# Attention and gated-MLP block in float32 pairs: the low-weight pass of a 64-channel rest as two 64-row matmuls on separate halves of the array

## The chip, the cores and the metric

The kernel runs on one core of a Trainium2 chip. The metric is the device time of one execution in microseconds (us). The kernel before was run three times: 1588.62 us median, 1587.64 lowest, 1589.95 highest.

The engines are TensorE (PE in the profile; its weight loads are listed apart as PEld), VectorE (DVE), ScalarE (ACT), GpSimd (POOL) and SyncE (SP, which issues most loads).

## The reference, cut to what matters

One transformer block over 2048 tokens of 576 channels, in float32:

```python
def reference(A_x, A_wqkv, A_wo, B_x, B_w_gate, B_w_up, B_w_down):
    def _A_ref(x, wqkv, wo):            # H = 32 heads of 18, window of 8 keys, dilation 2
        qkv = (x @ wqkv) ...            # x: (1, 2048, 576), wqkv: (576, 1728)
        idx = pos[:, None] - off[None, :]       # off = 0, 2, ..., 14; masked where negative
        logits = jnp.einsum("bhsd,bhswd->bhsw", q, kg) * scale
        attn = _softmax(logits, axis=-1)
        o = jnp.einsum("bhsw,bhswd->bhsd", attn, vg)
        return ... @ wo
    def _B_ref(x, w_gate, w_up, w_down):        # 576 -> 4608 -> 576
        return (sigmoid(x @ w_gate) * (x @ w_up)) @ w_down
    h = x + _A_ref(_layernorm(x), A_wqkv, A_wo)
    return h + _B_ref(_layernorm(h), B_w_gate, B_w_up, B_w_down)
```

## The kernel before

**Numbers as pairs.** A float32 matrix product is made of products of float32r parts. An operand is split (`split`, lines 103 to 105): ScalarE writes the rounded value `hi`, VectorE writes `lo`, the source less `hi`. A product is then hi times hi, lo times hi, and hi times lo; the product of the two low parts is left out.

**The rest of 64 channels.** The 576 channels are four chunks of 128 and a rest of 64. The rest is held twice, on rows 0 to 63 and on rows 64 to 127. For the tokens (`split_rest`, lines 107 to 109) ScalarE writes the rounded values to all 128 rows, and VectorE replaces rows 64 to 127 by the low parts: the fifth chunk of `th` is 64 rows of hi and 64 rows of lo. The weights are held twice as well, and `wh[:, 4]` and `wl[:, 4]` each have the same 64 rows on both halves. So one 128-row matmul of `th[:, 4]` with `wh[:, 4]` makes hi times hi and lo times hi together, and a second one with `wl[:, 4]` makes hi times lo, and lo times lo beside it.

**QKV.** The tokens are taken by parity (the window has dilation 2) and by half: four blocks of 512 tokens, each of four tiles of 128. The 32 heads are four groups, so the weights of a group are 576 by 432 (q, k and v of eight heads). `qkv(b, g, T, w)` (line 377) does one block and one group: for each of its four tiles, `tok_major` (line 144) makes 14 matmuls of 128 rows by 432 columns into one accumulator `acc` of PSUM, 12 for the four chunks (line 150), one with `wh[:, 4]` (line 152) and one with `wl[:, 4]` (line 153). ScalarE then copies the accumulator to `ev` (line 384), and after the fourth tile three DMAs on ScalarE's queue write q, k and v to DRAM (lines 388 to 390). There are 16 calls, 64 tiles. Five buffers `acc` are shared with the transposes of the layer norm's rest (`ln1`, line 349) and with the output projection.

**Order.** Everything is unrolled, and the order of each engine is settled when the program is built, from the program's order and from priorities (`tc.high_priority`). The generators are stepped by hand. `qkv` yields after each tile, and between two yields one or more steps of the attention (`att_all`, line 399) are taken, whose arithmetic is on VectorE: multiply by the keys (line 182), reduce (186), softmax, multiply by the values (208), adds (214 to 219). In the first blocks a tile of the layer norm is stepped as well, with five transposes on TensorE (139 and 143), a split on ScalarE and VectorE (104, 105) and one of the rest (108, 109).

The calls run in the order (block, group) (0,0), (0,1), (1,0), (2,0), (3,0), (1,1), (0,2), (2,1), (3,1), half of (1,2), (0,3), the other half, (2,2), (3,2), (1,3), and then half of (2,3). Behind the last matmul of that half (`passes[-1]`) the output projection of block 0 is started (`front`, `proj_j`): transposes of the attention's result `o`, a split, products with `wo`, the layer norm of the sum, transposes, splits, and a spill of the result to DRAM (`xscr[0]`, line 505). The other half of (2,3) and (3,3) are stepped between its parts.

**MLP.** Then come 36 hidden tiles of 128 for each pair of blocks, with matmuls of 512 columns (609, 616) and of 288 (723). The attention and projection of the other blocks go on under them.

Of the kernel before, what the change touches and what calls it, by code (L numbers as in the profile page):

```python
# [17 lines left out]
AF = mybir.ActivationFunctionType  # L18
ALU = mybir.AluOpType
AX = mybir.AxisListType  # L20

P = 128
# [8 lines left out]
NS = 4  # L31
# [7 lines left out]
NQ = 3 * CG  # L39
# [21 lines left out]
def kernel(ctx, tc, x, wqkv, wo, wmlp, out):  # L61
    nc = tc.nc
    dve, act, pool, pe, sp = nc.vector, nc.scalar, nc.gpsimd, nc.tensor, nc.sync
# [34 lines left out]
    def f32(ap):  # L98
        return ap.bitcast(F32)
# [3 lines left out]
    def split(hi, lo, src):  # L103
        act.activation(hi, src, AF.Copy)  # L104
        splits.append(dve.tensor_tensor(lo, src, f32(hi), ALU.subtract))  # L105

    def split_rest(t, src):
        act.activation(t, src, AF.Copy)
        dve.tensor_tensor(t[64:128], src[64:128], f32(t[64:128]), ALU.subtract)  # L109

    def pads(g):
        for e in range(2):
# [5 lines left out]
    def ln_j(xj, xn, on_act):  # L118
        bs = sm.tile([P, 2, 6], F32, bufs=4, name="bs")
        mv = sm.tile([P, 2], F32, bufs=4, name="mv")  # L120
        rstd = sm.tile([P, 1], F32, bufs=4, name="rstd")
        for k in range(2):
            dve.bn_stats(bs[:, k], xj[:, k * DH2:(k + 1) * DH2])
        dve.bn_aggr(mv, bs)
        dve.tensor_scalar(rstd, mv[:, 1:2], EPS, None, ALU.add)
        pool.tensor_tensor(rstd, rstd, mhalf, ALU.pow)
        if on_act:
            nm = sm.tile([P, 1], F32, bufs=4, name="nm")
            dve.tensor_scalar(nm, mv[:, 0:1], -1.0, None, ALU.mult)
            act.activation(xn[:, :D], xj, AF.Identity, bias=nm)  # L130
            act.activation(xn[:, :D], xn[:, :D], AF.Copy, scale=rstd)
            act.activation(xn[:, D:DX], xn[:, DM:D], AF.Copy)
        else:
            dve.tensor_scalar(xn[:, :D], xj, mv[:, 0:1], rstd, ALU.subtract, ALU.mult)
            dve.tensor_copy(xn[:, D:DX], xn[:, DM:D])

    def tr_main(ps, xn):
        for c in range(4):
            pe.transpose(ps[:, c * P:(c + 1) * P], xn[:, c * P:(c + 1) * P], ident)
        return ps.rearrange("p (c n) -> p c n", c=4)  # L140

    def tr_rest(ps, xn):
        pe.transpose(ps[:, :P], xn[:, DM:DX], ident)
        return ps[:, :P]

    def tok_major(ps, n, th, tl, js, wh, wl):
        k = 0
        for c in range(4):
            for a, m in ((th, wh), (tl, wh), (th, wl)):
                pe.matmul(ps[:, :n], a[:, c, js], m[:, c], start=k == 0, stop=False)  # L150
                k += 1
        pe.matmul(ps[:, :n], th[:, 4, js], wh[:, 4], start=False, stop=False)  # L152
        return pe.matmul(ps[:, :n], th[:, 4, js], wl[:, 4], start=False, stop=True)  # L153

    behind = [None]

# [83 lines left out]
    def proj_j(bank, t, wos, th, tl, xn_tile, put, order=(0, 1)):  # L240
        oj = t[0]
        pv = tr_main(bank(), oj)
        with tc.high_priority(HI):
            split(th[:, 0:4], tl, pv)
        yield
        pv = tr_rest(bank(), oj)
        with tc.high_priority(HI):
            split_rest(th[:, 4], pv)
        yield
        for i in order:  # L250
            ps = bank()
            tok_major(ps, DH2, th, tl, slice(0, P), *wos[i])
            hs = t[1][:, i * DH2:(i + 1) * DH2]
            with tc.high_priority(HI):
                dve.tensor_tensor(hs, hs, ps[:, :DH2], ALU.add)
            yield
        xn = xn_tile()
        with tc.high_priority(HI):
            ln_j(t[1], xn, False)
        yield  # L260
        pv = tr_main(bank(), xn)
        with tc.high_priority(HI):
            put(pv, slice(0, 4))
        yield
        pv = tr_rest(bank(), xn)
        with tc.high_priority(HI):
            put(pv.unsqueeze(1), slice(4, 5))
        yield
# [18 lines left out]
    def th_tile():  # L287
        return xt.tile([P, 5, TB], F32R, tag="th", bufs=3, name="th")

    def tl_tile():  # L290
        return xt.tile([P, 4, TB], F32R, tag="tl", bufs=4, name="tl")

    def x_half(raw, rest):
        t = tl_tile() if rest is None else th_tile()
        split(t[:, 0:2], t[:, 2:4], raw)
        if rest is not None:
            split_rest(t[:, 4], rest)
        return t
# [17 lines left out]
    def mm_tile():  # L316
        return psp.tile([P, 512], F32, tag="mm", bufs=3, name="mm")

    def acc_tile():
        return psp.tile([P, 512], F32, tag="acc", bufs=5, name="acc")  # L320

    def tok_tile(shape=(P, NS, DX)):
        return stk.tile(list(shape), F32, tag="tok", bufs=2, name="tok")

    def th3_tile(dt):
        return sar.tile([P, 5, TB], dt, tag="th3", name="th3")

    def ev_tile(shape):
        return sar.tile(shape, F32, tag="ev", bufs=2, name="ev")
# [8 lines left out]
    def ln1(b, xb):  # L338
        th = th3_tile(F32R) if b == 3 else th_tile()
        tl = tl_tile()  # L340
        yield th, tl
        xn = tok_tile()
        for j in range(NS):
            js = slice(j * P, (j + 1) * P)
            pri = 2 * HI if b == 0 else HI if b > 1 else 0
            with tc.high_priority(pri):
                ln_j(xb[:, j], xn[:, j], b > 1)
            pv = tr_main(mm_tile(), xn[:, j])
            pr = tr_rest(acc_tile(), xn[:, j])
            with tc.high_priority(pri):  # L350
                split(th[:, 0:4, js], tl[:, :, js], pv)
                split_rest(th[:, 4, js], pr)
            yield

    def raw_w(g):
        if g == 3:
            wr = sah.tile([P, NS, D], F32, bufs=2, name="h").rearrange("p j d -> p (j d)")
            wr = wr[:, :QC].rearrange("p (c n) -> p c n", c=5)
        else:
            wr = swo.tile([P, 5, NQ], F32, tag="wo", name="wr")  # L360
        for c in range(5):
            sp.dma_start(wr[:, c], wqkv[g][:, c * NQ:(c + 1) * NQ])
        return wr

    def qkv_w(g, wr=None):
        w = saw.tile([P, 2, 5, NQ], F32R, tag="qw", bufs=2, name="qw")
        for c in range(5):
            if wr is None:
                ws = sas.tile([P, NQ], F32, tag="wst", bufs=3, name="ws")
                sp.dma_start(ws, wqkv[g][:, c * NQ:(c + 1) * NQ])  # L370
            else:
                ws = wr[:, c]
            with tc.high_priority(3 * HI if g == 0 else HI):
                split(w[:, 0, c], w[:, 1, c], ws)
        return w

    def qkv(b, g, T, w):
        e, hf = BLOCKS[b]
        ev = ev_tile([P, 3, NS, CG])
        for j in range(NS):  # L380
            ps = acc_tile()
            passes.append(tok_major(ps, NQ, *T, slice(j * P, (j + 1) * P), w[:, 0], w[:, 1]))
            with tc.high_priority(HI):
                act.activation(ev[:, :, j], ps[:, :NQ].rearrange("p (t c) -> p t c", t=3), AF.Copy)  # L384
            yield
        r0 = LP + hf * TB
        with tc.high_priority(HI):
            act.dma_start(qscr[b][g], ev[:, 0].rearrange("p j c -> p (j c)"))
            for t, s in ((1, kscr), (2, vscr)):
                act.dma_start(s[e][g][r0:r0 + TB, :].rearrange("(p j) c -> p (j c)", p=P),  # L390
                              ev[:, t].rearrange("p j c -> p (j c)"))
        emitted.add((b, g))
# [4 lines left out]
    passes = []  # L397
# [24 lines left out]
    T = []  # L422

    def norm_under(b, xb, call, n):
        gl = ln1(b, xb)
        T.append(next(gl))
        for _ in call:
            step(ag, n)
            next(gl, END)
            step(ag, n)  # L430
        drain(gl)

    def heads(order, ws, n):
        for b, g in order:
            for _ in qkv(b, g, T[b], ws[g]):
                step(ag, n)

    xb = load_x(0)
    w = [qkv_w(0, raw_w(0))]
    gl = ln1(0, xb)  # L440
    T.append(next(gl))
    run(gl, qkv(0, 0, T[0], w[0]))
    w.append(qkv_w(1))
    xb = load_x(1)
    pads(0)
    norm_under(1, xb, qkv(0, 1, T[0], w[1]), 0)
    pads(1)
    xb = load_x(2)
# [79 lines left out]
    last = passes[-1]  # L528
# [376 lines left out]
    c = 0  # L905
# [204 lines left out]
    for c, (kind, p, f) in enumerate(items):  # L1110
        w, d = wc
# [116 lines left out]
```

## Time and profile before

| | |
|---|---|
| median of three runs | 1588.62 us |
| lowest, highest | 1587.64, 1589.95 us |
| profiled execution: span, first to last instruction | 1589.2 us (no other time is shown for it) |
| TensorE busy | 98% of the span, 8532 matmuls |
| VectorE, ScalarE, GpSimd busy | 80%, 55%, 12% |
| matmuls of line 150 into `acc`, `th` and `tl` against `qw` | 512 + 256, 155.7 + 92.8 us busy |
| matmuls of line 153 into `acc` against `qw` | 64, 23.0 us busy |
| first and last matmul of line 153 into `acc` against `qw` | 16.9 and 222.8 us |

In the rows below, L153 is line 153 of the kernel. A row of the timeline has the start, the time, the engine, the line, the operation, the tile written and the tiles read, the shapes and the count. A row of waits has the waiting engine and line, the one waited for, the total in us, the number of times and the longest. Matmuls overlap in the array, so the busy time of a group isn't its cost, and the recorded times of single matmuls add up to more than the time that passes.

### The profile page before, as it was taken

What the parts mean: (1) busy time and instruction counts of PE and PEld (TensorE: products, weight loads), DVE (VectorE), ACT (ScalarE), POOL (GpSimd) and SP (SyncE); (2) the same over time, 40 slices, a digit from 0 to 9 for tenths busy, and PEclk for the clock granted to TensorE, in tenths of its full rate; (3) what the DMA queues carried; (4) which work ended last, traced back from release to release, by engine and by line L of the source; (5) the groups of instructions that cost most, each with busy time, mean ns of one, the idle gap of its engine ahead of it and who ended that gap; (6) DMA issues with size and microseconds to landing.
All of it is one profiled execution on the core that took longest, in us unless ns stands there. A gap on an engine that the chain in (4) does not pass through costs nothing.

```text
span 1589.2 us, 22383 instructions
## 1 busy us (share of the span) xinstructions
PE 1553.3 (98%) x8532; PEld 1381.6 (87%) x8532; DVE 1268.1 (80%) x1931; ACT 869.2 (55%) x1546; POOL 184.2 (12%) x230
## 2 busy tenths in 40 slices
PE   7999979999999999999989999999999999999998
PEld 6999968888888888888879988888888888888887
DVE  7999988959999999999546687876677776677755
ACT  4432234425555666656443255776677776677761
POOL 1000000011010001000101100122112112212210
PEclk9999999999999999999999999999999999999999
DMA  7664544346367565665764234899989999989983
GB/s 267 208 206 163 193 184 165 133 177 246 104 164 205 157 170 139 166 191 149 210 203 143 100 110 110 182 186 181 176 169 183 184 173 180 177 170 182 184 170 124
DMA packets 76892, 273.50 MB, mean 172 GB/s; under 512 B 8336, under 2 KB 14224, under 8 KB 75888
## 3 DMA queue, kind: packets, MB, share of 16 engines
q0 software_dynamic: 27792, 105.89, 36.3%
q1 hardware_dynamic: 41360, 146.06, 27.4%
q10 hardware_dynamic: 7632, 20.12, 3.3%
q8 instruction: 67, 1.10, 0.3%
q14 instruction: 41, 0.34, 0.1%
HBM read 145.88 MB, written 128.52 MB: 173 GB/s over the span
## 4 chain that ended last, share of the span: by engine, by line
PE 55%; issue 27%; POOL 7%; DVE 6%; DMA 4%; ACT 1%; SPq 0%; POOLq 0%; ACTq 0%; DVEq 0%
PE b L609 23%; PE dp L723 15%; POOL h L794 7%; PE acc L150 6%; PE b L616 4%; PE b L150 1%; PE bgp L150 1%; DMA wg<-in_wmlp_dram 1%; DVE pr L182 1%; DMA x<-tok 1%; DVE pr L208 1%; DVE lg L186 1%; PE acc L152 1%; DMA tail<-h 1%; PE acc L153 1%
## 5 line engine op out<-in xcount | busy, mean ns | idle before, releaser
L609 PE MATMUL b<-tl,w 128*128 128x512 f32 x1716 | 438.1, 395 | 9.1 <-ACT w L104 6.5
L609 PEld LDWEIGHTS b<-tl,w 128*128 128x128 f32 x1716 | 311.7, 189 | 66.5 <-ACT w L104 7.7
L609 PE MATMUL b<-th,w 128*128 128x512 f32 x1368 | 352.8, 393 | 0.4 <-DVE s L698 0.3
L609 PEld LDWEIGHTS b<-th,w 128*128 128x128 f32 x1368 | 249.8, 188 | 46.7 <-DVE s L698 0.7
L104 ACT ACTIVATE w<-wg 128x640 fp32r<-128x640 f32 (+2 forms) x197 | 117.0, 598 | 125.2 <-PE b L616 59.8
L791 ACT ACTIVATE ev<-dp 128x576 f32<-128x576 f32 x224 | 145.0, 647 | 61.8 <-PE dp L785 58.2
L616 PE MATMUL b<-th,w 128*128 128x512 f32 x572 | 177.0, 391 | 0.0
L794 POOL DMA_DIRECT2D h<-ev x128 | 110.2, 862 | 456.8 <-ACT ev L791 440.5
L105 DVE TENSOR_TENSOR w<-wg,w 128x640 fp32r<-128x640 f32 (+2 forms) x197 | 126.8, 649 | 38.7 <-ACT w L104 38.3
L150 PE MATMUL acc<-qw,th 128*128 128x432 f32 x512 | 155.7, 365 | 1.2 <-DVE th L109 0.9
L105 DVE TENSOR_TENSOR w<-tw,w 128x512 fp32r<-128x512 f32 x116 | 79.6, 687 | 81.1 <-ACT w L104 80.2
L616 PEld LDWEIGHTS b<-th,w 128*128 128x128 f32 x572 | 107.7, 188 | 23.1
L723 PE MATMUL dp<-d,h0h 128*128 128x288 f32 x640 | 119.0, 296 | 1.7 <-DVE tail L733 1.7
L723 PE MATMUL dp<-d,h1h 128*128 128x288 f32 x640 | 120.0, 297 | 0.0
L723 PEld LDWEIGHTS dp<-d,h0h 128*128 128x128 f32 x640 | 99.4, 189 | 5.5 <-DVE tail L733 2.0
L150 PEld LDWEIGHTS acc<-qw,th 128*128 128x128 f32 x512 | 97.2, 190 | 6.5 <-DVE th L109 1.1
L723 PEld LDWEIGHTS dp<-d,h1h 128*128 128x128 f32 x640 | 99.5, 190 | 2.9
L731 ACT ACTIVATE stage<-dp 128x576 f32<-128x576 f32 x96 | 61.7, 646 | 62.4 <-PE dp L723 62.3
L104 ACT ACTIVATE w<-tw 128x512 fp32r<-128x512 f32 x116 | 72.8, 628 | 41.3 <-PE b L609 40.9
L150 PE MATMUL acc<-qw,tl 128*128 128x432 f32 x256 | 92.8, 362 | 0.0
L384 ACT ACTIVATE ev<-acc 128x432 f32<-128x432 f32 x64 | 33.9, 531 | 104.4 <-PE acc L153 97.7
L182 DVE TENSOR_TENSOR pr<-kw,q 128x2304 f32<-128x2304 f32 x32 | 81.7, 2552 | 2.8 <-DMA kw<-k 2.6
(278 smaller groups left out, 2899.8 us busy)
## 6 DMA issues: line engine op xcount, KB each, us to landing
h<-ev POOLq DMA_DIRECT2D x96, 576.0 KB, 7.2
wg<-in_wmlp_dram SPq DMA_DIRECT2D x49, 928.0 KB, 5.2
h<-stage POOLq DMA_DIRECT2D x24, 1152.0 KB, 10.6
wg<-in_wmlp_dram SPq DMA_DIRECT2D x36, 640.0 KB, 4.1
kw<-k SPq DMA_DIRECT2D x16, 792.0 KB, 4.4
vw<-v SPq DMA_DIRECT2D x16, 792.0 KB, 5.5
wd<-in_wmlp_dram SPq DMA_DIRECT2D x18, 576.0 KB, 7.2
h<-ev POOLq DMA_DIRECT2D x32, 288.0 KB, 6.8
```

Source lines behind the costliest of these rows:

```text
L104: act.activation(hi, src, AF.Copy)
L105: splits.append(dve.tensor_tensor(lo, src, f32(hi), ALU.subtract))
L150: pe.matmul(ps[:, :n], a[:, c, js], m[:, c], start=k == 0, stop=False)
L152: pe.matmul(ps[:, :n], th[:, 4, js], wh[:, 4], start=False, stop=False)
L182: dve.tensor_tensor(pr, both(kw, u), q[:, us].unsqueeze(2).broadcast_to([P, 2, W, CG]), ALU.mult)
L384: act.activation(ev[:, :, j], ps[:, :NQ].rearrange("p (t c) -> p t c", t=3), AF.Copy)
L609: pe.matmul(ps, wt[:, a, k0 + c], xx[:, m + c], start=first and k == 0, stop=k == 5, skip_group_check=True)
L616: pe.matmul(ps, wt[:, a, k0], xx[:, 4], start=False, stop=a == 1, skip_group_check=True)
L723: pe.matmul(ps[:, i, :DH2], a[:, js], d[:, m, i * DH2:(i + 1) * DH2], start=k == 0, stop=k == n)
L731: act.activation(hv, ps, AF.Copy)
L791: act.activation(hs[:, k % 2], ps[:, :, :DH2], AF.Copy)
L794: pool.dma_start(hsev[:, u, k0:k + 1], hs[:, :k + 1 - k0], accum_op=ALU.add, max_dma_last_dim=8 * D)
```

## The change

The tiles of a `qkv` call are taken as two couples. For each tile of a couple there are the 12 matmuls of the chunks and the one with `wh[:, 4]` as before; behind those of both tiles come two matmuls with `wl[:, 4]`, one for each tile, of 64 rows: rows 0 to 63 for the first tile, rows 64 to 127 for the second. Each reads only the rows that hold hi of its tile, so for odd tiles `split_rest` writes the low parts to rows 0 to 63 instead. The product lo times lo of the rest, which the 128-row matmul made beside the other, is no longer made. The two accumulators of a couple are allocated together, and both are copied out behind the couple's last matmul. `qkv` still yields four times.

```diff
-    def split_rest(t, src):
+    def split_rest(t, src, low=1):
         act.activation(t, src, AF.Copy)
-        dve.tensor_tensor(t[64:128], src[64:128], f32(t[64:128]), ALU.subtract)
+        r = slice(64 * low, 64 * low + 64)
+        dve.tensor_tensor(t[r], src[r], f32(t[r]), ALU.subtract)
...
+    def tok_pair(pp, n, th, tl, jj, wh, wl):
+        for ps, js in zip(pp, jj):
+            k = 0
+            for c in range(4):
+                for a, m in ((th, wh), (tl, wh), (th, wl)):
+                    pe.matmul(ps[:, :n], a[:, c, js], m[:, c], start=k == 0, stop=False)
+                    k += 1
+            pe.matmul(ps[:, :n], th[:, 4, js], wh[:, 4], start=False, stop=False)
+            yield
+        for i in range(2):
+            r = slice(64 * i, 64 * i + 64)
+            last = pe.matmul(pp[i][:, :n], th[r, 4, jj[i]], wl[r, 4], start=False, stop=True)
+        yield last
...
-                split_rest(th[:, 4, js], pr)
+                split_rest(th[:, 4, js], pr, 1 - j % 2)
...
-        for j in range(NS):
-            ps = acc_tile()
-            passes.append(tok_major(ps, NQ, *T, slice(j * P, (j + 1) * P), w[:, 0], w[:, 1]))
+        for j in range(0, NS, 2):
+            pp = [acc_tile() for _ in range(2)]
+            jj = [slice((j + i) * P, (j + i + 1) * P) for i in range(2)]
+            half = tok_pair(pp, NQ, *T, jj, w[:, 0], w[:, 1])
+            next(half)
+            yield
+            next(half)
+            passes.append(next(half))
             with tc.high_priority(HI):
-                act.activation(ev[:, :, j], ps[:, :NQ].rearrange("p (t c) -> p t c", t=3), AF.Copy)
+                for i in range(2):
+                    act.activation(ev[:, :, j + i],
+                                   pp[i][:, :NQ].rearrange("p (t c) -> p t c", t=3), AF.Copy)
             yield
```

## The prediction

> **What bounds the kernel now.** I read the page first (busy shares, slices, the chain that ended last), then the windows of the first 300 us, the waits of TensorE in them, the two instructions that the change splits (lines 152 and 153), and the timeline around single matmuls.
>
> ```profile
> span 1589.2 us, 22383 instructions
> PE 1553.3 (98%) x8532; PEld 1381.6 (87%) x8532; DVE 1268.1 (80%) x1931; ACT 869.2 (55%) x1546; POOL 184.2 (12%) x230
> PE   7999979999999999999989999999999999999998
> PE 55%; issue 27%; POOL 7%; DVE 6%; DMA 4%; ACT 1%; SPq 0%; POOLq 0%; ACTq 0%; DVEq 0%
> ```
>
> TensorE is the bound almost everywhere: 98% busy, and the chain runs over it. The low slices are the first, and the sixth (200 to 240 us). So a delay that leaves the QKV stage late goes on to the end one for one, unless one of the few idle places takes it up. Those are in the windows (columns: stretch, length, busy us and count of PE, PEld, DVE, ACT, POOL, then clock, DMA) and in TensorE's waits up to 300 us:
>
> ```profile
> 40.00:50.00 10.00, 9.14 (x54) 8.49 (x53) 9.72 (x29) 6.75 (x16) 2.20 (x4) 1.00 0.90 322
> 50.00:60.00 10.00, 9.74 (x57) 8.93 (x56) 9.72 (x12) 7.02 (x17) 0.00 (x0) 1.00 0.60 184
> 130.00:140.00 10.00, 10.00 (x53) 9.56 (x52) 9.86 (x6) 1.60 (x3) 0.91 (x1) 1.00 0.10 30
> 180.00:190.00 10.00, 8.67 (x59) 8.17 (x58) 9.84 (x17) 3.72 (x10) 0.00 (x0) 1.00 1.00 360
> 230.00:240.00 10.00, 1.46 (x3) 0.78 (x4) 6.86 (x5) 6.15 (x10) 0.00 (x0) 0.61 0.55 223
> ```
>
> ```profile
> PE mm L150 <- DVE tl L105: 1.3, 1, 1.3
> PE acc L150 <- DVE th L109: 0.9, 1, 0.9
> PE acc L150 <- ACT ev L384: 0.3, 1, 0.3
> PE acc L152 <- DVE th L109: 0.3, 1, 0.3
> ```
>
> In the QKV stage TensorE has no gap (10.00 of 10 at 130 us), and VectorE is nearly as full beside it (9.86), with the attention of the heads that are ready. TensorE waits for VectorE's splits at 40 to 60 us (0.9 + 0.3 = 1.2 us) and once at 187 us (1.3 us).
>
> **What one low-weight matmul costs.** A matmul's recorded time is its way through the array; what it costs in a full stream is the distance from start to start.
>
> ```profile
> L153 PEld LDWEIGHTS acc<-qw,th x64: 187/188/330, 16.5 to 222.6; 128*128 128x128 f32 x64
> L153 PE MATMUL acc<-qw,th x64: 352/357/542, 16.9 to 222.8; 128*128 128x432 f32 x64
> ```
>
> ```profile
> 131.25 0.36 PE L150 MATMUL acc<-qw,th 128*128 128x432 f32 x1
> 131.45 0.36 PE L152 MATMUL acc<-qw,th 128*128 128x432 f32 x1
> 131.64 0.36 PE L153 MATMUL acc<-qw,th 128*128 128x432 f32 x1
> 131.84 0.36 PE L150 MATMUL acc<-qw,th 128*128 128x432 f32 x1
> ...
> 189.43 0.30 PE L152 MATMUL mm<-wo,th 128*128 128x288 f32 x1
> 189.56 0.30 PE L153 MATMUL mm<-wo,th 128*128 128x288 f32 x1
> 189.69 0.29 PE L150 MATMUL mm<-wo,th 128*128 128x288 f32 x1
> ```
>
> At 432 columns a matmul recorded at 0.36 us costs 0.59/3 = 0.197 us. The weight load beside it, 0.188 us by its record, isn't what sets this: at 288 columns, with the same 128 weight columns, the distance is 0.13 us. So the load is hidden, and the columns streamed are what costs.
>
> **The change, part by part.** There are 64 token tiles (16 calls of four), so 32 couples. Each loses two 128-row matmuls of 432 columns and gets two 64-row ones of 432. Halving the rows doesn't shorten the stream; only both halves streaming at once does. If they overlap wholly, a couple saves one distance, 0.197 us, 32 x 0.197 = 6.3 us over the kernel: that is all there is to win.
>
> Against it stand two changes of shape in each couple: 128 rows to 64 ahead of the couple's last two matmuls, and back to 128 behind them. No row here has a matmul on fewer than 128 rows, so I bound the price. The nearest rows are a change of kind in a running stream, and a start out of an empty array:
>
> ```profile
> 218.54 0.36 PE L150 MATMUL acc<-qw,tl 128*128 128x432 f32 x1
> 218.74 0.27 PE L143 MATMUL acc<-ident,tok 128*128 128x128 f32 x1
> 218.77 0.45 PE L150 MATMUL acc<-qw,th 128*128 128x432 f32 x1
> 219.05 0.27 PE L143 MATMUL acc<-ident,tok 128*128 128x128 f32 x1
> ...
> 220.11 0.46 PE L150 MATMUL acc<-qw,th 128*128 128x432 f32 x1 [0.28 <-ACT ev L384]
> 220.41 0.36 PE L150 MATMUL acc<-qw,tl 128*128 128x432 f32 x1
> 220.60 0.55 PE L150 MATMUL acc<-qw,th 128*128 128x432 f32 x2
> ```
>
> A transpose and a matmul take 219.05 - 218.74 = 0.31 us together, 0.11 more than the matmul alone: a change of kind by itself empties nothing. The start after a wait costs 0.30 us to the next matmul (220.11 to 220.41) where 0.20 is usual: 0.10 us of weight load that nothing covers.
>
> Bounds for a couple, from the start of its last 128-row matmul (zero) to the second 128-row matmul after it, which is at 4 x 0.197 = 0.79 us now. Nothing emptied, halves together: 0.79 - 0.20 = 0.59, a gain of 0.20. Array emptied at both changes, weights loaded meanwhile: halves start at 0.36, end at 0.72, the next starts there, the second at 0.92: a loss of 0.13. Array emptied and every load after it in the open: the first half at 0.36, the second 0.10 later at 0.46, ending 0.46 + 0.46 = 0.92, the next there, the second 0.30 later at 1.22: a loss of 0.43. [...] Whether loads go on meanwhile no row tells, so I take the middle of the two, a loss of 0.28 us, nearest to the start after a wait; both ends stay in the range.
>
> The Trainium skill, TensorEngine Tiling (Array Packing), section Tiling Modes, says that a change of tiling mode, not of tile alone, drains TensorE; no run here shows it. By that rule the gain of 0.20 falls out of the bounds above.
>
> The sum. The first 14 calls and the first couple of the fifteenth stand ahead of the output projection, which starts at 184 us: 29 couples; three are mixed into it.
>
> ```profile
> 184.04 0.71 PE L139 MATMUL mm<-ident,tok 128*128 128x128 f32 x5
> 187.73 0.40 PE L150 MATMUL mm<-wo,th 128*128 128x288 f32 x1 [1.33 <-DVE tl L105]
> ```
>
> ```profile
> 180.86 0.76 DVE L219 TENSOR_TENSOR tok<-kw 128x576 f32<-128x576 f32 x1
> 181.53 2.55 DVE L182 TENSOR_TENSOR pr<-kw,q 128x2304 f32<-128x2304 f32 x1
> 184.41 2.54 DVE L186 TENSOR_REDUCE lg<-pr 128x128 f32<-128x2304 f32 x1
> 186.98 0.69 DVE L105 TENSOR_TENSOR tl<-mm,th 128x512 fp32r<-128x512 f32 x1
> ```
>
> 29 x 0.28 = 8.1 us late at 184 us, less 1.2 us of idle at 40 to 60, less 1.3 us at 187, where TensorE now waits for a split that stands behind a 2.54 us reduction on VectorE: 5.6 us. Behind it the projection's last transposes lead to the spill that holds the next stage back (the chain in order of time, and a wait of ScalarE):
>
> ```profile
> 221.19 11.15 DMA x<-tok
> ACT d L104 <- DMA x<-tok: 8.7, 1, 8.7
> ```
>
> TensorE sits idle for 8.5 of the 10 us at 230 behind it. The three couples mixed in add 3 x 0.28 = 0.8 us ahead of that spill. Together 6.4 us, carried to the end by a full TensorE: 1589.2 + 6.4 = 1595.6 against the profiled span. The median of the three runs (1588.62) is 0.6 lower, so the forecast is 1595.0.
>
> The rest I put at nothing. The half-tile subtraction of odd tiles (line 109) has the same shape on the other 64 rows. The couple's two evictions (line 384) queue together on ScalarE, which is at 1.60 of 10 us busy: the first comes one tile later, the last one eviction later, and q, k and v with it; the attention reads them calls later. A couple holds two of five accumulators until its end; where transposes take others between its halves, TensorE could meet an unevicted one, for which it waits 0.3 us in all now; without that cover an eviction for each couple of the four calls that share with the norm is under 8 x 0.5 = 4 us, in the range. The order of instructions is settled when the program is built, and could move one attention operation, 2.5 us, to either side of the projection's splits: plus or minus 2.5 us.
>
> **The rivals.** *Halves overlap, nothing empties.* TensorE would be 29 x 0.197 = 5.7 us early at 184 us. But o is finished by line 219 at 180.86 + 0.76 = 181.6, and the split at 186.98 stands behind VectorE's reduction: VectorE was 9.8 of 10 us busy and did not wait for TensorE. If its order stays, the early arrival is waited away at 187 and the time is 1588; if the splits slip ahead of the reduction, 2.5 us come out, 1586; if all came through, with the last three couples, 1588.6 - 6.3 = 1582.3. Over 0.2% (3.2 us) faster needs VectorE's order to move by more than one operation. The Trainium skill, TensorE: Matmul & The Clock Gate, Part 3, has matmuls on different row groups start about 4 ns apart, which would be this rival's gain; nothing here shows it.
>
> *Full price.* Every load in the open: 29 x 0.43 = 12.5, less 2.5, plus 1.3 = 11.3 us, 1599.9. For it speaks the start at 220.11; against it, that loads otherwise run ahead of the stream.
>
> *Nothing moves.* The halves run one behind the other and no change of shape costs anything, so the edit does not do what it says (0 us), or the array empties with all loads hidden: 29 x 0.13 = 3.8, less 2.5, plus 0.4 = 1.7 us. 1588.6 to 1590.3. The transpose row speaks for the first: a change of kind in the stream cost only its own load.
>
> **How the numbers follow.** Forecast (half the loads hidden, +4 to +9 us) 0.38; full price or more 0.22; nothing moves 0.22; overlap without emptying 0.18. What a measurement of this kernel can tell from no change is about 0.2%, 3.2 us; the three runs spread over 2.3. Slower by more: 0.38 + 0.22, 0.60. Faster by more: most of the overlap case with the order moved in its favour, 0.15. Within: 0.25. The range runs from 1584, most of the overlap gain, to 1604, the full price with the waits for accumulators; the slow cases alone give 1592 to 1604.
>
> **What would show it.** In the profile after: lines with 64-row tiles, their two starts close together (0.1 us or less) if they overlap; 0.36 us or more from the last 128-row matmul to the first half, and again behind the second, if the array empties; the projection's transposes at about 191 us instead of 184; the spill of x at about 227 instead of 221; the rest of the kernel shifted whole. I am wrong if the distances around the halves stay at 0.20 us, if the projection starts at 184 or sooner, or if delays ahead of it are made up for later.

## The result, and the profile after

The changed kernel takes 1592.99 us (median of 20 runs, 1589.26 to 1597.33) and the kernel before, on the same chip, 1590.57 us (20 runs, 1587.64 to 1593.01). The ratio is 1.0016, with a 95% interval of 1.0009 to 1.0024: 2.4 us slower, clear of no change, and less than the 0.2% that I had called the limit.

```profile
span 1588.0 us, 22384 instructions
PE 1557.5 (98%) x8532; PEld 1371.4 (86%) x8532; DVE 1267.3 (80%) x1931; ACT 868.0 (55%) x1546; POOL 184.1 (12%) x230
```

The span of this profile is shorter than that of before (1589.2), against the medians. Its own time was 1590.2 us, 2.2 over its span, and that is 2.8 under the median of its kernel; the execution shown of before, with the same 2.2 us, stood at 1591.4, 0.8 over its median. So the two spans can't be set against each other, and I compare stages. In the timeline of TensorE, this is what became of a couple's end:

```profile
125.95 0.36 PE L163 MATMUL acc<-qw,th 128*128 128x432 f32 x1
126.24 0.46 PE L167 MATMUL acc<-qw,th 64*128 64x432 f32 x2
126.63 0.47 PE L161 MATMUL acc<-qw,th 128*128 128x432 f32 x1
126.93 0.36 PE L161 MATMUL acc<-qw,tl 128*128 128x432 f32 x1
```

```profile
126.24 0.19 PEld L167 LDWEIGHTS acc<-qw,th 64*128 64x128 f32 x2 [0.29 <-issue]
126.63 0.19 PEld L161 LDWEIGHTS acc<-qw,th 128*128 128x128 f32 x1 [0.20 <-issue]
```

The two halves together take the 0.46 us that a single one takes: they start 0.003 us apart (all starts of the trace, median of 23 couples) and stream at once, and so do their two weight loads. But the first half starts 0.29 us behind the last full matmul, the next full one 0.39 us behind the half, and the one after it 0.30 us later, where 0.196 is usual; and the loads, which otherwise run ahead, start together with their matmuls. Summed: 0.985 us from the last full matmul to the second after the halves, where four distances of 0.196 are 0.78. One distance was to be saved, and one is lost.

So it is in 28 of the 32 couples. In the other four the order as it was built puts other work between the two halves (they start at 17 and 22 us, 45 and 48, 55 and 56, 224 and 227), so eight halves stand alone, and each pays its own way there and back. This is the last couple, with a transpose and 13 full matmuls of the second tile in between:

```profile
223.64 0.46 PE L167 MATMUL acc<-qw,th 64*128 64x432 f32 x1
224.03 0.33 PE L144 MATMUL acc<-ident,tok 128*128 128x128 f32 x1
...
226.91 0.46 PE L167 MATMUL acc<-qw,th 64*128 64x432 f32 x1
```

The busy time of the engines by stretches of 10 us, to be set beside those of before in the prediction:

```profile
40.00:50.00 10.00, 9.51 (x51) 7.76 (x50) 9.78 (x31) 6.59 (x15) 2.20 (x4) 1.00 0.90 330
50.00:60.00 10.00, 10.00 (x55) 8.66 (x55) 9.87 (x13) 6.38 (x17) 0.00 (x0) 1.00 0.78 266
130.00:140.00 10.00, 10.00 (x51) 8.66 (x50) 9.90 (x8) 1.91 (x4) 0.91 (x1) 1.00 0.43 155
180.00:190.00 10.00, 10.00 (x55) 8.70 (x54) 9.93 (x11) 1.22 (x3) 0.00 (x0) 1.00 0.69 232
230.00:240.00 10.00, 3.94 (x18) 2.93 (x16) 7.53 (x5) 2.63 (x4) 0.00 (x0) 0.90 0.91 367
240.00:250.00 10.00, 8.93 (x30) 6.78 (x31) 7.77 (x14) 6.65 (x12) 0.00 (x0) 0.75 0.28 98
```

At 130 us 51 matmuls go into 10 us instead of 53, and TensorE's idle time at 180 us is gone. The projection and the MLP begin later:

```profile
189.04 0.77 PE L140 MATMUL mm<-ident,tok 128*128 128x128 f32 x5
227.30 1.65 PE L631 MATMUL b<-tl,wf 128*128 128x512 f32 x6
```

That is 5.0 us later for the projection (184.04 before), and 4.35 for the MLP: in before its first matmul started at 222.95. Nothing is left of this lead for before by 355 us, in these two executions. I follow it by the start of the same hidden-tile matmul, counted through, in both traces, after less before: +4.3 us at the first, +0.9 at the 100th (263 us), +1.0 at 298, -2.2 at 355, -1.3 from 930 to 1540, -0.1 at the last one. So something gives back 3.4 us between 223 and 263, and 3.2 between 298 and 355. TensorE's waits from 222 to 360 us, after and then before:

```profile
PE b L631 <- ACT w L104: 6.8, 1, 6.8
PE b L140 <- DMA oj<-o: 0.8, 1, 0.8
PE b L631 <- DVE w L105: 0.4, 1, 0.4
PE b L631 <- DVE s L651: 0.3, 1, 0.3
```

```profile
PE b L609 <- ACT w L104: 6.5, 1, 6.5
PE b L609 <- DVE s L629: 2.5, 1, 2.5
PE b L139 <- DMA oj<-o: 2.4, 1, 2.4
```

Two waits shrank: one for VectorE behind the spill of x (2.5 to 0.3) and one for the load of the attention's result (2.4 to 0.8). Neither is a wait for a half-row matmul. The waits up to 263 us add up to 9.0 us in before (6.5 + 2.5) and 7.5 in after (6.8 + 0.4 + 0.3), which is 1.5 of the 3.4 us; the rest is matmuls at a lower clock, to which the swap below comes back.

### The profile page after: what moved, and what is told of

Same layout as the page of the kernel before. It is cut to its first block, busy times and chain, and to the rows that moved or that the text cites. A ratio compares the mean times of both kernels' runs of the same rounds, so it can differ in the third digit from the quotient of the medians.

```text
span 1588.0 us, 22384 instructions
## 1 busy us (share of the span) xinstructions
PE 1557.5 (98%) x8532; PEld 1371.4 (86%) x8532; DVE 1267.3 (80%) x1931; ACT 868.0 (55%) x1546; POOL 184.1 (12%) x230
## 4 chain that ended last, share of the span: by engine, by line
PE 89%; DVE 4%; DMA 4%; issue 1%; ACT 1%; SPq 0%; POOL 0%; POOLq 0%; DVEq 0%; ACTq 0%
PE b L631 41%; PE dp L745 14%; PE dp L807 11%; PE acc L161 9%; PE b L638 8%; DMA wg<-in_wmlp_dram 3%; PE b L151 1%; PE bgp L151 1%; PE acc L167 1%; PE acc L163 1%; DMA tail<-h 1%; DVE w L105 1%; DVE tl L105 0%; PE mm L140 0%; PE b L140 0%
## 5 line engine op out<-in xcount | busy, mean ns | idle before, releaser
L223 DVE TENSOR_TENSOR pr<-vw,lg 128x2304 f32<-128x2304 f32 x32 | 81.8, 2555 | 0.7
```

What stands on the lines that cost most here:

```text
L223: dve.tensor_tensor(pr.rearrange("p j w (h d) -> p j w h d", d=DH), both(vw, u).rearrange("p j w (h d) -> p j w h d", d=DH), lg[:, us].uns ...
```

## The experiments

The question is twofold: is the loss in the QKV stage the price of the changes of shape, or of the couples; and what gives time back behind it?

**Couples on all rows.** Only the row halves are undone. The orders of VectorE's and ScalarE's instructions are those of the changed kernel.

```diff
-            r = slice(64 * i, 64 * i + 64)
-            last = pe.matmul(pp[i][:, :n], th[r, 4, jj[i]], wl[r, 4], start=False, stop=True)
+            last = pe.matmul(pp[i][:, :n], th[:, 4, jj[i]], wl[:, 4], start=False, stop=True)
```

> The changed kernel with one thing undone: the couple's two low-weight matmuls are on all 128 rows again (432 columns each); couples, paired evictions and the halves of the rest stay. VectorE's order is that of the changed kernel. Theory A (the loss is the price of going from 128 rows to 64 and back, 0.195 us a couple as the trace of after has it; the regain behind the QKV stage comes from VectorE's changed order): distances of 0.20 us throughout, the MLP's first matmul at 223.0 us (after: 227.3), and the end 4 to 6 us ahead of after's, 1587 to 1589 against 1590.6 before, so faster than both. Rival B (the regain is a delay that the idle stretch at 230 to 240 us takes up, whatever the order): MLP's first matmul at 223.0, but the end at that of before, 1590.6 within 1. Rival C (the couples, not the rows, cost: two accumulators held, evictions late): the MLP's first matmul stays at 226 to 227 and the time at 1593.

Measured: 1586.67 us, ratio to before 0.9970 (0.9959 to 0.9982). It beats both kernels. In its timeline the couple's two stand in the stream like any others:

```profile
132.03 0.36 PE L163 MATMUL acc<-qw,th 128*128 128x432 f32 x1
132.23 0.55 PE L166 MATMUL acc<-qw,th 128*128 128x432 f32 x2
132.62 0.36 PE L161 MATMUL acc<-qw,th 128*128 128x432 f32 x1
...
220.05 1.55 PE L630 MATMUL b<-tl,wf 128*128 128x512 f32 x6
```

The MLP starts at 220.05 us, 7.25 ahead of after and, which theory A had not foreseen, 2.9 ahead of before. So the halves cost some 7 us of the QKV stage. Between 60 and 182 us, where every couple has its halves together, after falls back by 4.4 us in 22 couples, 0.20 each (0.985 less 0.781 here); the 2.6 us ahead of that arise in seven couples, three of them with separated halves. The couples by themselves gain 2.9. (In two later experiments TensorE's order up to the MLP is that of before and of this kernel, and the MLP starts at 223.63 and 220.88, so such a difference is good to 0.8 us.) Rival C is out. The medians agree: 1592.99 - 1586.67 = 6.3 us for the halves, and 3.7 less than the 1590.41 of before, measured beside it, for all else in the change. Behind the MLP's start this kernel gains too: -2.9 at the first hidden-tile matmul becomes -6.4 at 263 us, the same 3.5 us as in after with a start 7.25 us later. That is against rival B, by which a delay would be what is taken up.

**Both halves on the same rows.**

```diff
-            r = slice(64 * i, 64 * i + 64)
+            r = slice(0, 64)
...
-                split_rest(th[:, 4, js], pr, 1 - j % 2)
+                split_rest(th[:, 4, js], pr)
```

> The changed kernel, but both low-weight matmuls of a couple are on rows 0 to 63 (and the rest's halves are as in the kernel before), so they can't stream at once. VectorE's order is that of after. Theory A (the two halves overlap wholly, and the two changes of shape cost 0.39 us a couple): the second half starts 0.18 to 0.20 us behind the first instead of 0.003, the couple costs 1.18 us from the last full matmul to the second after it where after has 0.985 and before 0.79; MLP's first matmul at 227.3 + 32 x 0.197 - 0.2 = 233.4, the time 6 us above after's, 1599. Rival (the halves overlap only in their records; each streams alone in after already): distances and time as after, 1593.

Measured: 1596.32 us, ratio 1.0033 (1.0024 to 1.0043).

```profile
134.78 0.35 PE L163 MATMUL acc<-qw,th 128*128 128x432 f32 x1
135.06 0.65 PE L167 MATMUL acc<-qw,th 64*128 64x432 f32 x2
135.65 0.47 PE L161 MATMUL acc<-qw,th 128*128 128x432 f32 x1
135.95 0.36 PE L161 MATMUL acc<-qw,tl 128*128 128x432 f32 x1
```

The two now take 0.65 us in the record instead of 0.46, the sum is 1.177 us (1.18 expected), and the MLP starts at 232.78 (233.4 expected). So the overlap in after is real and is worth what it should be. One detail is off: the second half starts 0.305 us behind the first, not 0.20, and the way back is 0.28 instead of 0.39. A 64-row load isn't wholly hidden behind a matmul on the same rows, as a 128-row load is. The end, 3.3 us above after by the medians and 2.7 under the 1599 expected, is less than the 5.5 by which the MLP starts later; in the one trace the later hidden-tile matmuls stand 6 to 9 us behind those of after, 6.1 at the last. That execution of after is 2.8 us under its median, and this one 0.1 over its own, so the trace and the medians agree.

**One half for each tile.** The kernel before with its low-weight matmul on 64 rows; VectorE's order is that of before.

```diff
-        return pe.matmul(ps[:, :n], th[:, 4, js], wl[:, 4], start=False, stop=True)
+        return pe.matmul(ps[:, :n], th[:rows, 4, js], wl[:rows, 4], start=False, stop=True)
```

> The kernel before, with each tile's low-weight matmul on rows 0 to 63 alone, where it stands (no couples; low times low of the rest is left out as in the change). 64 lone halves, so 128 changes of shape. VectorE's order is exactly that of before. Theory A: 0.29 + 0.39 + 0.30 = 0.98 us from the last full matmul to the second after the half, against 0.59 in before: 0.39 a tile, 64 x 0.39 = 25 us in the QKV stage, less 2.5 that idle places take: MLP's first matmul at 245 to 247. With VectorE's order that of before there is no regain behind it, so the time is 1590.6 + 22.5 = 1613. Rival B (the idle stretch at 230 to 240 takes delays up): 3 to 5 us less, 1608 to 1610. Rival D (a row-tiled matmul by itself costs nothing, the couple's evictions do): 1590.6.

Measured: 1609.65 us, ratio 1.0119 (1.0103 to 1.0134).

```profile
132.03 0.36 PE L152 MATMUL acc<-qw,th 128*128 128x432 f32 x1
132.32 0.46 PE L153 MATMUL acc<-qw,th 64*128 64x432 f32 x1
132.71 0.46 PE L150 MATMUL acc<-qw,th 128*128 128x432 f32 x1
133.01 0.36 PE L150 MATMUL acc<-qw,tl 128*128 128x432 f32 x1
```

The distances are 0.29, 0.39 and 0.30, as with a pair: there and back costs 0.39 us more than the stream, whether one half or two stand in between. The MLP starts at 243.84 us, 20.9 late (22 to 24 expected); at 263 us of before's time it is 19.0 late, and 19.1 at the last hidden-tile matmul. With before's order of VectorE the stretch behind the start gives back 1.9 us of 20.9, where the couples' order gives back 3.4 to 3.6 at three different starts (4.3 late, 2.9 early, and 9.8 late in the kernel with both halves on the same rows). The time, though, is 3.4 us under theory A's 1613 and in the range of rival B: idle places took up 4.1 of the 25 us ahead of the MLP, where I had 2.5, and 1.9 behind its start, where I had nothing. So that idle time takes up some of a long delay isn't excluded here.

**The pair issued twice.**

```diff
-        for i in range(2):
+        for k in range(4):
+            i = k % 2
...
-            last = pe.matmul(pp[i][:, :n], th[r, 4, jj[i]], wl[r, 4], start=False, stop=True)
+            last = pe.matmul(pp[i][:, :n], th[r, 4, jj[i]], wl[r, 4], start=False, stop=k > 1)
```

> The changed kernel with the couple's pair of halves issued twice in a row, so hi times low weights of the rest is added twice. No change of shape is added, only one more pair per couple. Theory A (the pair streams at once, and the price sits in the changes of shape): one matmul distance more, 0.197 us a couple, 6.3 us in all: MLP's first matmul at 233.4, the time 1599. Rival (each half costs its own stream, or each weight load on half the rows is in the open): 0.39 to 0.5 us a couple, 12.6 to 16 us: MLP's first matmul at 240 or later, 1605 to 1609.

Measured: 1591.37 us, ratio 1.0001 (0.9993 to 1.0010). The sum is 1.18 us instead of 0.985, one distance more, as theory A has it, and the MLP starts at 234.79 (233.4 expected), 11.8 us behind before. The time, though, is that of before, 8 us under what I expected. The trace gives back 7.9 us by 263 us and 3.6 more by 355. Behind the MLP's start, this is the spill of x and TensorE's wait for the weight splits:

```profile
232.56 6.00 DMA x<-tok
PE b L632 <- ACT w L104: 0.7, 1, 0.7
```

The spill takes 6.0 us from issue to landing, against 9.5 to 11.2 in the ten other traces, and the wait is 0.7 us, against 6.8 in after. So here the idle stretch did take up most of the delay, as rival B of the first experiment has it. This kernel's order of VectorE and ScalarE is another again, and why its spill lands sooner isn't shown. Theory A's price of a pair holds, and its tacit step from the price to the end does not.

**Four tiles behind one change of shape.** In 13 calls `tok_pair` gets four tiles and ends with four halves, two on each half of the rows, and the norm's transposes of the rest go to `mm` buffers. In the trace ten of the 13 end with four halves in a row; in the other three the order as built puts other work between them.

```diff
-        for j in range(0, NS, 2):
-            pp = [acc_tile() for _ in range(2)]
+        many = 2 if (b, g) in ((1, 2), (2, 3), (3, 3)) else NS
+        for j in range(0, NS, many):
+            pp = [acc_tile() for _ in range(many)]
```

> The changed kernel with four token tiles instead of two behind one change of shape, in 13 of the 16 calls (the calls that are interrupted or mixed with the output projection stay in couples): four 64-row matmuls in a row, two on each half. The transposes of the rest of the norm take the other three PSUM buffers. Theory A (the changes of shape cost, and a second pair costs one matmul distance; with the pair issued twice the distances were 0.283, 0.003, 0.301, 0.003, 0.285, 0.303 us, 1.18 in all): 1.18 us from the last full matmul to the second after the four, where full matmuls take 6 x 0.196 = 1.18: no gain and no loss in these calls, 0.2 us lost in each of the six couples left. First MLP matmul at 220 + 1.2 = 221.3 us, 1 or 2 later if the transposes wait for buffers; time 1587 to 1589. Rival (every pair of halves costs 0.2 us whatever stands around it): first MLP matmul at 227, time 1593.

Measured: 1589.87 us, ratio 0.9994 (0.9985 to 1.0003). The sum of a row of four is 1.186 us: no gain, no loss, as expected. Against the couples on all rows TensorE is 1.5 us late at 64 us and 2.0 late at 171: nearly level in the stream between. But the MLP starts at 229.74, 8 us later than I forecast. The waits of TensorE in the first 232 us show the reason:

```profile
PE acc L144 <- DVE tok L433: 4.3, 1, 4.3
PE mm L140 <- DVE tok L234: 0.8, 1, 0.8
```

These are the projection's transposes waiting for the attention's result and its copies on VectorE. Here VectorE, not TensorE, sets when the projection goes on: the limit that I had named for the gaining rival. Behind the long wait the granted clock is lower as well, 0.83 on the mean of 180 to 200 us, where it is 1.00 in after.

**Before, with one swap.** The first split of the down weights is written in the MLP's first hidden tile. TensorE's order is untouched; VectorE has one attention product ahead of that split instead of behind it, and ScalarE issues the write-out of v ahead of it.

```diff
-        split(d[:, 0], d[:, 1], wg[:, GU:WC])
         wc = ww, d
+    d0, wg0 = d, wg
...
+        if c == 0:
+            with tc.high_priority(HI):
+                split(d0[:, 0], d0[:, 1], wg0[:, GU:WC])
```

> The kernel before with one swap: the first split of the down weights (ScalarE's copy and VectorE's subtraction into d) is written in the first hidden tile of the MLP instead of ahead of it, which puts one 2.55 us attention product ahead of it on VectorE, as in the changed kernel's order, and one instruction ahead of it on ScalarE. TensorE's order is unchanged. Theory A (the 3.5 us that the changed kernel and the couples on all rows regain between 223 and 263 us come from this order): first MLP matmul at 223.0 as before, TensorE's wait of 2.5 us for VectorE at 239.8 falls to under 0.6, the slow clock behind it is shorter, and the 60th hidden-tile matmul comes 2.5 to 3.5 us sooner; time 1587 to 1588. Rival (the regain is from something else that the couples changed, such as the accumulators or the evictions): 1590.4 as before.

Measured: 1588.57 us, ratio 0.9992 (0.9983 to 1.0001): 2.1 us under before, with no change just inside the interval. VectorE in the stretch, first before, then with the swap:

```profile
226.19 2.55 DVE L186 TENSOR_REDUCE lg<-pr 128x128 f32<-128x2304 f32 x1
233.08 0.76 DVE L105 TENSOR_TENSOR d<-wg,d 128x576 fp32r<-128x576 f32 x1 [4.34 <-ACT d L104]
233.75 2.55 DVE L182 TENSOR_TENSOR pr<-kw,q 128x2304 f32<-128x2304 f32 x1
236.34 2.55 DVE L186 TENSOR_REDUCE lg<-pr 128x128 f32<-128x2304 f32 x1
238.92 0.69 DVE L629 TENSOR_TENSOR s<-s,b 128x512 f32<-128x512 f32 x1
```

```profile
229.43 2.56 DVE L182 TENSOR_TENSOR pr<-kw,q 128x2304 f32<-128x2304 f32 x1
233.65 0.76 DVE L105 TENSOR_TENSOR d<-wg,d 128x576 fp32r<-128x576 f32 x1 [1.66 <-ACT d L104]
234.32 2.55 DVE L186 TENSOR_REDUCE lg<-pr 128x128 f32<-128x2304 f32 x1
236.90 0.69 DVE L629 TENSOR_TENSOR s<-s,b 128x512 f32<-128x512 f32 x1
```

The subtraction into d waits for ScalarE, which waits for the spill of x. In before VectorE idles 4.34 us in front of it and then does 5.1 us of attention while TensorE needs s (gate times up); with the swap 2.56 us of it fall into the idle time, and TensorE's wait of 2.5 us for s is gone. But a wait of 0.8 us for ScalarE (h0h, the rounded s, behind two splits) comes up in its place, and the lag falls by 1.4 us by 263 us (+0.7 to -0.7), not by 3.5. So the swap explains part of what is regained there. It shortens TensorE's waits as much as the change does (9.0 to 7.4 us); the clock is the rest, as far as the traces show it. In before the granted clock is 0.61 at 230 to 240 and this at 240 to 250:

```profile
240.00:250.00 10.00, 10.00 (x33) 8.04 (x34) 6.15 (x12) 3.62 (x7) 0.00 (x0) 0.70 0.29 95
```

In the trace that is half clock from 232.3 to 246.0 us, 13.7 us. TensorE idles through 6.2 of them (to 236.0, and the 2.5 for s) and works in 7.4. In after (0.90 and 0.75, above) the half clock lasts 6.8 us, from 238.1 to 244.9, and TensorE works in some 3.8. Half of the difference in work, 1.8 us, is about what the waits leave of the 3.4. With the swap the half clock lasts 10.2 us. What sets its length isn't shown: it is 10.2 us too in the kernel with one half for each tile, where TensorE stops for 2.3 us, and in one of the further traces of after, where it stops for 0.6 at most.

**Couples on all rows, the split later still.** The same edit with the split in the second hidden tile (`c == 1`).

> The couples with the low-weight pass on all 128 rows, and the first split of the down weights written one hidden tile later still, so that VectorE runs the attention's product, reduction and maximum in the time in which that split waits for the spill of x. Theory A (what VectorE does in the idle stretch is what is regained): VectorE's idle time of 1.9 us before that split goes, TensorE's start after the stretch is bound by ScalarE's weight splits alone; up to 1.5 us more than the couples on all rows, 1585 to 1586.7. Rival (the stretch is bound by the spill's landing and the weight splits, and VectorE is no longer late): 1586.7, the same.

Measured: 1584.84 us, ratio 0.9961 (0.9948 to 0.9975), the fastest here, 1.8 us under the couples on all rows by the medians; the two intervals overlap, so the further gain isn't settled. Nor does it come from the stretch: there the trace gives back 3.4 us (2.1 early at the MLP's first matmul, 5.5 at 263 us), no more than the couples on all rows, as the rival has it. VectorE's wait ahead of the split into d goes, but one of 1.77 us for ScalarE ahead of a split into w comes up, and TensorE waits 7.5 us for ScalarE's weight splits, where it was 7.1. The lead over the couples on all rows grows behind that, to 2.1 us from 930 us on, and the edit doesn't explain it.

**The changed kernel profiled twice more.** Is the short wait for the attention's load at 314 us one execution's luck?

> The changed kernel again, one look. Its first profile had a span of 1588.0 us (its time 1590.2, the median 1593.0) and a wait of 0.8 us for the load of the attention's result at 314 us, where seven other profiles show a wait of 2.0 to 2.7 us or, in two kernels that are later there by other amounts, 0.7 and 0.9, with 3.4 us of half clock behind the long one. Theory E (that wait differs from execution to execution): this one shows 2.0 to 2.7 us, and a span of 1590 to 1592, with the first MLP matmul at 227.3 and the 60 to 200th as before within 1 us of the first look. Rival F (it belongs to the kernel's order and lateness): 0.8 us again.

> The changed kernel a third time, for the same question: by theory E (the wait of 0.8 us at 314 us differs by execution) at least one of the two looks shows 2.0 us or more and half clock behind it; by rival F (it belongs to the kernel) both show 0.7 to 1.0 us and no half clock there.

Measured: spans of 1589.6 and 1588.6 us, waits of 1.1 and 0.6 us, no half clock behind them. Of the other eight traces six wait 2.0 to 2.7 us and two 0.7 and 0.9. Theory E's forecast failed in both: in three traces of three this kernel waits briefly, and it gives back 2.6 and 3.2 us there in the two new ones. But the three executions (1590.2, 1591.8 and 1590.8 us) are all under the kernel's median of 1593.0, so that its slower executions wait as briefly isn't shown. What decides the wait stays open. Neither lateness alone nor VectorE's order does: the couples on all rows (2.5 us) and both halves on the same rows (2.7 us) share VectorE's order with after and wait long, one earlier and one later than it.

## Why the prediction was right, and where it was not

**The mechanism held.** The array does not pass from 128 rows to 64 and back for nothing, the halves do overlap, and the price is above the gain. The Trainium skill, TensorEngine Tiling (Array Packing), section Tiling Modes, says that changing the mode drains TensorE: the trace agrees, with 0.39 us there and back above the usual distances. The other rule weighed, that of the Trainium skill, TensorE: Matmul & The Clock Gate, Part 3, with starts about 4 ns apart on different row groups, agrees as well: 3 ns. Both are true at once; the second one's gain of 0.196 us is half of the first one's cost.

**The price was mis-sized.** I took a loss of 0.28 us a couple, the middle of 0.13 and 0.43; it is 0.20. Of the two bounds neither picture is right: the array's wait into the half is only 0.09 us beyond the stream (I had 0.16), and the open load costs on the way back. With 0.20 my sum gives 29 x 0.20 = 5.8, less 2.5, plus 0.6: 3.9 us instead of 6.4. That the array empties I took ahead of any row that shows it. And I had counted on 32 couples with their halves together, where four came apart.

**The absorption was near.** TensorE's idle time at 187 us went, as forecast, and the projection began 5.0 us late, where 5.8 - 1.2 = 4.6 would follow from the true price. That they are so near is luck: against the couples on all rows (181.80) the halves had cost 7.2 us by then, more than 5.8 for the separated ones, and the couples themselves had gained 2.2. The MLP began 4.35 us late, 7.25 for the halves less the couples' 2.9.

**The step that failed is the one for the rest, which I put at nothing, and with it the carry to the end.** The couples themselves are worth 2.9 us by the MLP's start: in the kernel with couples on all rows TensorE's waits for VectorE's splits of the rest fall from 1.2 to 0.2 us, and the one at 187 us from 1.3 to 0.6; all its waits up to there add up to 2.2 us less (14.1 to 11.9), and the rest of the 2.9 isn't traced. In the stretch from 223 to 263 us the new order of the engines gives back 3.4 us more, of which VectorE's order around one split explains 1.4. I had named that stretch only as a place where TensorE idles behind the spill, and had bounded a shifted attention operation at 2.5 us, to either side of the projection's splits; it fell on the first split of the MLP instead, and the half clock was shorter there. I had looked for accumulators held too long, a loss; TensorE's wait for ScalarE's evictions was 0.3 us before and is none after. My last sign of being wrong, delays that are made up for later, is what came: +4.3 us at the MLP's start and nothing left by 355 us in the trace, and 2.4 us at the end by the medians where the sum had 6.4. The rise is real, but smaller than the 0.2% above which I had put 0.60; that the time lies well inside the range owes as much to these two gains, which I had not seen, as to the price.

**The rival with the gain** was wrong about emptying, but its limit is real: in the kernel with four tiles to a change of shape TensorE waits 4.3 us for the attention.

**What stays open:** the wait at 314 us, what the slower executions of after do differently, what sets the length of the half clock, and why the spill of x lands sooner where the pair is issued twice.

## What to carry to other kernels

Half-row matmuls pay only in runs: in float32r at 432 columns, there and back costs two matmul distances, so one pair loses one, two pairs break even, and by that sum a gain needs more than two (not run here). Whether the pairs are still together is seen only in the trace: the order as built can part them. An edit that changes how work is grouped also changes every engine's order, and that can be worth more than the edit; undo the disputed instruction alone and keep the grouping, as here, where the grouping was the gain (0.9970) and the instruction the loss. In a stretch where an engine waits for a transfer, look at what stands behind the waiting instruction in its queue: work that could have filled the wait may make the next engine late, as it did here for 2.5 us.

## What the runs showed of the hardware

Two 64-row matmuls on different halves start 3 ns apart and load their weights at once. Weight loads of 64 rows on the same rows as the running matmul are in part in the open: 0.305 us from start to start, against 0.196 for full ones, whose loads are hidden. Behind 6.5 to 6.8 us of idle time TensorE went on at half clock for a time that differed between traces: the half clock lasted 13.7 us in before, where TensorE stopped again for 2.5 us, and 6.8 us in after.
